# Fourier mixing gated with a dense Mish layer: fourteen additions of a loaded tile become accumulating transfers

## The chip, the core and the metric

The kernel runs on one core of a Trainium2 chip. The metric is device time in microseconds (us), median of several runs of the whole program. Engines are named as in the profile: PE (TensorE matmul), PEld (its weight load), DVE (VectorE), ACT (ScalarE), POOL (GpSimd), SP (SyncE). On-chip tiles live in SBUF; matmuls write to eight PSUM banks. Transfers are issued by SP (nearly all loads, and the stores of the output) and by POOL (the stores of intermediate results).

## The reference

```python
a = einsum("bsd,ed->bse", x, dft_hid_re);  b = einsum("bsd,ed->bse", x, dft_hid_im)
A = einsum("ts,bse->bte", dft_seq_re, a) - einsum("ts,bse->bte", dft_seq_im, b)
h = einsum("bsd,df->bsf", x, w1) + b1
B = einsum("bsf,fd->bsd", h * tanh(softplus(h)), w2)        # Mish
g = sigmoid((x * gate_w).sum(-1, keepdims=True))
out = g * A + (1 - g) * B
```

x is 2048 tokens by 640; the hidden size of the dense layer is 1728. All is float32.

## The kernel before

All results are kept transposed: rows are features (five blocks of 128, called d = 0 to 4), columns are tokens (four blocks of 512, called t = 0 to 3). A tile of 128 x 512 floats is 256 KB. Every matmul of float32 operands is three matmuls of operands that are split in a high and a low part (`mm3`, line 325); `operand` (line 313) makes the split, the high part on ACT (line 315), the low part on DVE (line 316). There are ten pairs of operand tiles (r0 to r9).

The stages come in this order. The sequence transform (`sq`) leaves u in DRAM. The hidden transform (`hd`) multiplies it by the gate g and leaves g y in DRAM: the scratch `ysc[d][t]`, twenty tiles, shown as `y` in the profile. The first dense layer leaves the activations in DRAM (`asc`, shown as `act`). The last stage (`ou`, weights `w2`) multiplies the activations, adds g y, and stores `out`. Each of these products is a 2 x 2 block scheme with seven block products in place of eight (class `Problem`, line 391), for two token blocks at a time, with the fifth feature block beside it:

- `first` computes the block product that others start from, and for the second pair of token blocks puts it by in DRAM (`aside`, shown as `po`) until it is needed;
- `second` runs the products called 22, s2 and s1 over six steps k, after a remainder of the contraction (`rest`);
- `third` runs 12, s3 and s4 over six steps, and gives the results.

The last stage has two such problems. In problem 0 (t = 0 and 1) the results leave PSUM in `done` and `give`, multiplied by 1 - g (`q`), and `plus` (line 541) then adds a loaded tile of g y to each of its ten results: line 543, a load and a DVE addition. In problem 1 (t = 2 and 3) the activations were scaled by 1 - g already, so g y is added on the way: `add_y` (line 474) adds it as a PSUM bank is emptied (six tiles), and four tiles are added to partial sums in SBUF that were read back from `po`: line 427 for the fifth block of t = 3, lines 455 to 457 for two tiles, and line 461 for the fifth block of t = 2. These four partial sums are then copied by ACT into a PSUM bank (`copy`, line 296), on which later matmuls accumulate. Additions are the helper `tt`, whose line is 288.

Nothing of the order is written out by hand but that of the matmuls. The program is collected as a graph (`Graph.add`), the matmuls in the order of the calls; `Graph.run` then plans the other engines by list scheduling: due times are worked back from the matmuls, each instruction has a modelled duration, and of the instructions that are ready the one that is due first goes next, if a tile can be granted from its pool (`FS`: 18 tiles f, to which the six tiles x are added when the stages that use them are through). A transfer is modelled as 2.2 us and its size at 370 KB per us. The result is one fixed order for each engine and each queue, and a tile for each value. On the chip every queue runs in that order: an instruction that waits holds up all behind it on its queue.

Of the kernel before, what the change touches and what calls it, by code (L numbers as in the profile page):

```python
# [12 lines left out]
OP = mybir.AluOpType  # L13

S, D, F = 2048, 640, 1728
P = 128
N = 512
# [202 lines left out]
def fnet_mish_gate(ctx: ExitStack, tc: tile.TileContext, xn, xt, c_re, c_im, wd_re, wd_im,  # L220
                   w1a, w1b, b1a, b1b, w2, gw, out):
    nc = tc.nc
# [10 lines left out]
    FS = Pool("f", [sb.tile([P, N], F32, name=f"f{i}") for i in range(NFS)])  # L233
# [11 lines left out]
    def scratch(name, n, rows=P):  # L245
        return [[dram(f"{name}{i}_{t}", rows) for t in range(TG)] for i in range(n)]

    usc, ysc = scratch("u", 2 * KD), scratch("y", KD)
# [6 lines left out]
    def whole(*vals):  # L255
        return [(v, None) for v in vals]

    def dve(emit, r, w, n=N, more=0.0):
        took = 0.15 + n / 960 + more
        return G.add("DVE", emit, r, w, took, took - 0.083)  # L260
# [5 lines left out]
    def dma(queue, emit, r, w, size):  # L266
        op = G.add(queue, emit, r, w, DELAY + size / RATE, 0.605 if queue == "SP" else 1.0)
        op.moves = size / RATE
        return op
# [3 lines left out]
    def load(pool, src, of=None, rows=P, cols=N, queue="SP"):  # L273
        v = Val(pool)
        dma(queue, lambda: ISSUE[queue].dma_start(v.t[:rows, :cols], src() if callable(src) else src),
            whole(of) if of else [], whole(v), rows * cols * 4)
        return v

    def load_of(pool, d, rows=P):
        return load(pool, lambda: d.t, d, rows)  # L280

    def store(d, v, rows=P, queue=None):
        queue = queue or STORES
        dma(queue, lambda: ISSUE[queue].dma_start(d.t, v.t[:rows]), whole(v), whole(d), rows * N * 4)  # L284

    def tt(o, a, b, op, cut=(slice(None),) * 3, rows=slice(None), n=N):
        (x, y, z) = cut
        dve(lambda: nc.vector.tensor_tensor(o.t[rows, x], a.t[rows, y], b.t[rows, z], op=op),  # L288
            whole(a, b), whole(o), n)

    def fresh(pool, a, b, op):
        o = Val(pool)
        tt(o, a, b, op)
        return o

    def copy(o, a, scale=1.0):
        act(lambda: nc.scalar.activation(o.t, a.t, AF.Copy, scale=scale), whole(a), whole(o))  # L297
        return o

    def to_sbuf(bank):  # L300
        return copy(Val(FS), bank)
# [11 lines left out]
    def operand(src, pool=None):  # L313
        r = Val(pool or R)
        act(lambda: nc.scalar.activation(r.t[0][:, :N], src.t[:, :N], AF.Copy), whole(src), [(r, 0)])  # L315
        dve(lambda: nc.vector.tensor_tensor(r.t[1][:, :N], src.t[:, :N], f32(r.t[0][:, :N]), op=OP.subtract),  # L316
            whole(src) + [(r, 0)], [(r, 1)])
        return r
# [12 lines left out]
    def product(banks, blocks, x, start, stop):  # L331
        for bank, b in zip(banks, blocks):
            mm3(bank, b, x, start, stop)

    def bank():
        return Val(psum)
# [3 lines left out]
    class Stage:  # L340
# [25 lines left out]
        def low(self, k):  # L366
            if k in self.XB:
                return
            f, g, t = load(X, self.row(k)[:, :N]), load(X, self.row(k + self.kh), cols=D), Val(X)
            if self.neg:  # L370
                copy(g, g, -1.0)
            tt(f, f, f, OP.subtract, (A2, B2, A2), n=2 * P)
            tt(t, g, f, OP.subtract, (A2, B2, A2), n=2 * P)
            tt(f, f, g, OP.subtract, (B2, B2, B2), n=2 * P)
            tt(t, g, t, OP.subtract, (B2, A2, A2), n=2 * P)
            self.top(k)
            if k // KD not in self.T2:
                self.T2[k // KD] = Val(W)
            b, c = self.XB[k], self.XT13[k] = Val(W), Val(W)
            split(self.XA[k], 3, t, 2 * P, 2 * P)  # L380
            split(c, 4, t, 0, P)
            split(self.T2[k // KD], k % KD, t, P, P)
            split(c, 0, f)
            split(b, 0, g, 0, D)

    def in_turn(kh, begin, between, end):
        order = [(p, k) for p in begin for k in (0, 1)]
        order += [(p, k) for k in range(2, kh - 2) for p in between]
        return order + [(p, k) for p in end for k in (kh - 2, kh - 1)]

    class Problem:
# [25 lines left out]
        def second(self, low):  # L417
            st, kh, t1, t2, y = self.st, self.st.kh, self.t1, self.t2, self.y
            own = {}
            if self.aside:  # L420
                self.p1 = [load_of(FS, d) for d in self.aside[:2]]
                self.d = load_of(FS, self.aside[2])
                self.a = [copy(bank(), v) for v in self.p1]
            d2 = self.d
            if y:
                d2 = y(4, t2)
                tt(d2, d2, self.d, OP.add)
            self.d2 = copy(bank(), d2)
            p4, b = [bank(), bank()], [bank(), bank()]
            opened = False  # L430
            if self.rest:
                e = [bank(), bank()]
                self.rest(t2, e + p4 + [self.d2], (2, 3, 0, 1, 4), 4)
                opened = True
                r22 = [self.add_y(v, y, 2 + j, t2) for j, v in enumerate(e)]
            for p, k in in_turn(kh, *[("22", "s2", "s1")] * 3):
                if p == "22":
                    low(k)
                    a22, a21, a11 = self.moving(t2, k + kh), self.moving(t2, k), self.moving(t1, k)
                    tt(a21, a21, a22, OP.add)  # L440
                    tt(a11, a21, a11, OP.subtract)
                    own.update({("22", k): a22, ("s1", k): a21, ("s2", k): a11})
                x = operand(own.pop((p, k)))
                if p == "22":
                    product(p4, st.blocks("t4", k), x, k == 0 and not opened, k == kh - 1)
                    product([self.d2], st.blocks("low5", k), x, False, k == kh - 1)
                elif p == "s2":
                    product(self.a, st.t2(k), x, False, k == kh - 1)
                else:
                    product(b, st.blocks("t1", k), x, k == 0, k == kh - 1)  # L450
                if k < kh - 1:
                    continue
                if p == "22":
                    self.p4 = [self.add_y(v, y, j, t2) for j, v in enumerate(p4)]
                    if y:
                        for j, v in enumerate(self.p1):
                            tt(v, v, y(j, t1), OP.add)
                    self.c = [copy(bank(), v) for v in self.p1]
                    if self.aside:
                        if y:  # L460
                            tt(self.d, self.d, y(4, t1), OP.add)
                        self.d1 = copy(bank(), self.d)
                elif p == "s2":
                    u2 = [self.add_y(v, y, 2 + j, t1) for j, v in enumerate(self.a)]
                else:
                    self.p5 = [to_sbuf(v) for v in b]
                    for v, u in zip(b, u2):
                        tt(v, v, u, OP.add)
                    if self.rest:
                        for v, r in zip(self.p5, r22):  # L470
                            tt(v, v, r, OP.add)
            self.b = b
# [67 lines left out]

        def plus(self, f, d, t):
            if self.st is fin and not self.y:
                tt(f, f, load_of(FS, ysc[d][t]), OP.add)
            self.finish(d, t, f)

        def end(self):
# [252 lines left out]
    def put_out(d, t, f, queue=None):  # L799
# [8 lines left out]
                  y=(lambda d, t: load_of(FS, ysc[d][t])) if tp else None,  # L808
# [78 lines left out]
```

## Time and profile before

| | us |
|---|---|
| median of 3 runs | 868.31 (867.33 to 868.6) |
| the profiled execution, its own time | 868.39 |
| its span, first to last instruction | 866.6 |
| PE busy | 859.3 |
| DVE busy | 679.0 |
| ACT busy | 463.1 |
| POOL busy | 69.7 |

The profile tells busy time by engine, groups of instructions, who waited for whom, the chain of work that ended last, and the instructions by time. Matmuls follow one another every 0.23 us while each is shown as 0.39 us long, as they overlap; an idle gap stands in square brackets with what ended it. A DMA issue is shown on its queue (SPq, POOLq, ACTq), and its landing is told in the view of DMA issues. The last stage runs from about 694 us to the end; its problem 0 ends, and problem 1 goes on to its `second` part, at about 788 us, and to its `third` part at 824 us.

### The profile page before, as it was taken

How to read it: one execution, taken by the hardware profiler on the slowest of the kernel's cores; microseconds unless marked ns; L12 is line 12 of the kernel's file. 1: busy time of each engine (PE TensorE's matmuls, PEld its weight loads, DVE VectorE, ACT ScalarE, POOL GpSimd, SP SyncE). 2: the span in 40 equal slices, each digit the busy share in tenths (PEclk: the TensorE clock that was granted, in tenths of full speed). 3: DMA queues.
4: the chain of work that ended last, by engine and by line, in shares of the span. 5: the costliest groups of instructions: out<-in, count | busy, mean ns of one | idle time of the engine just before them, and what ended most of it. 6: DMA issues, size and time to landing. Idle time of an engine off the chain costs nothing.

```text
span 866.6 us, 11980 instructions
## 1 busy us (share of the span) xinstructions
PE 859.3 (99%) x3772; PEld 709.0 (82%) x3772; DVE 679.0 (78%) x1213; ACT 463.1 (53%) x849; POOL 69.7 (8%) x132
## 2 busy tenths in 40 slices
PE   9999999999999999999999999999999999999998
PEld 7888888888888878888888888888888888887786
DVE  7999958876785577999999899925576897739991
ACT  7765536544553544667473666745655764521541
POOL 0000002001000200002002012111222100000000
PEclk9999999999999999999999999999999999999999
DMA  9976749564955565679975959455363778526943
GB/s 331 340 274 233 271 148 344 197 211 136 356 177 189 188 242 182 217 270 339 370 267 210 331 207 362 166 195 203 126 211 137 263 274 287 185 84 209 377 161 121
DMA packets 103231, 203.50 MB, mean 235 GB/s; under 512 B 12800, under 2 KB 15232, under 8 KB 103168
## 3 DMA queue, kind: packets, MB, share of 16 engines
q1 hardware_dynamic: 92912, 169.57, 57.1%
q0 software_dynamic: 10112, 33.04, 10.3%
q8 instruction: 29, 0.48, 0.2%
q14 instruction: 34, 0.28, 0.1%
q10 hardware_dynamic: 144, 0.13, 0.0%
HBM read 164.40 MB, written 38.29 MB: 234 GB/s over the span
## 4 chain that ended last, share of the span: by engine, by line
PE 96%; DVE 1%; DMA 1%; ACT 1%; issue 0%; ACTq 0%; DVEq 0%
PE ps L321 96%; DVE f L288 1%; DMA x<-po 1%; PE ps L744 0%; DMA out_dram<-f 0%; DVE x L288 0%; ACT ps L297 0%; ACT r5h L315 0%; DVE r9l L316 0%; DVE r7l L316 0%; ACT r4h L315 0%; ACT r9h L315 0%; ACT r3h L315 0%; DVE r1l L316 0%; ACT r6h L315 0%
## 5 line engine op out<-in xcount | busy, mean ns | idle before, releaser
L288 DVE TENSOR_TENSOR f<-f,f 128x512 f32<-128x512 f32 x311 | 209.1, 685 | 10.7 <-DMA f<-u 3.5
L288 DVE TENSOR_TENSOR f<-ps,f 128x512 f32<-128x512 f32 x101 | 66.0, 685 | 43.3 <-PE ps L321 43.0
L297 ACT ACTIVATE f<-ps 128x512 f32<-128x512 f32 x128 | 74.9, 595 | 38.9 <-PE ps L321 30.4
L284 POOL DMA_DIRECT2D u<-f x40 | 21.6, 543 | 322.7 <-DVE f L288 310.1
L315 ACT ACTIVATE r3h<-f 128x512 fp32r<-128x512 f32 x43 | 27.1, 629 | 30.0 <-PE ps L321 17.8
L315 ACT ACTIVATE r2h<-f 128x512 fp32r<-128x512 f32 x40 | 25.2, 631 | 32.4 <-PE ps L321 23.7
L579 ACT ACTIVATE f<-f,b1s 128x512 f32<-128x512 f32 x36 | 25.7, 723 | 29.1 <-DVE f L288 29.0
L316 DVE TENSOR_TENSOR r9l<-f,r9h 128x512 fp32r<-128x512 f32 x41 | 28.2, 688 | 14.8 <-ACT r9h L315 14.4
L315 ACT ACTIVATE r1h<-f 128x512 fp32r<-128x512 f32 x38 | 23.9, 630 | 29.2 <-PE ps L321 19.0
L284 POOL DMA_DIRECT2D act<-f x52 | 28.3, 545 | 133.6 <-DVE f L288 71.0
L315 ACT ACTIVATE r8h<-f 128x512 fp32r<-128x512 f32 x40 | 25.2, 631 | 25.4 <-PE ps L321 18.0
L315 ACT ACTIVATE r9h<-f 128x512 fp32r<-128x512 f32 x41 | 25.8, 628 | 23.2 <-PE ps L321 19.0
L315 ACT ACTIVATE r0h<-f 128x512 fp32r<-128x512 f32 x40 | 25.1, 628 | 23.8 <-PE ps L321 18.1
L316 DVE TENSOR_TENSOR r2l<-f,r2h 128x512 fp32r<-128x512 f32 x40 | 27.6, 689 | 12.3 <-ACT r2h L315 12.0
L316 DVE TENSOR_TENSOR r7l<-f,r7h 128x512 fp32r<-128x512 f32 x39 | 26.8, 688 | 12.8 <-ACT r7h L315 12.5
L315 ACT ACTIVATE r6h<-f 128x512 fp32r<-128x512 f32 x39 | 24.5, 629 | 22.7 <-PE ps L321 16.4
L315 ACT ACTIVATE r7h<-f 128x512 fp32r<-128x512 f32 x39 | 24.5, 629 | 22.6 <-PE ps L321 16.1
L315 ACT ACTIVATE r5h<-f 128x512 fp32r<-128x512 f32 x40 | 25.1, 629 | 20.0 <-PE ps L321 14.1
L316 DVE TENSOR_TENSOR r0l<-f,r0h 128x512 fp32r<-128x512 f32 x40 | 27.5, 688 | 10.5 <-ACT r0h L315 10.2
L316 DVE TENSOR_TENSOR r5l<-f,r5h 128x512 fp32r<-128x512 f32 x40 | 27.5, 688 | 10.2 <-ACT r5h L315 8.2
L316 DVE TENSOR_TENSOR r8l<-f,r8h 128x512 fp32r<-128x512 f32 x40 | 27.5, 688 | 9.8 <-ACT r8h L315 9.5
L315 ACT ACTIVATE r4h<-f 128x512 fp32r<-128x512 f32 x37 | 23.3, 629 | 21.4 <-PE ps L321 20.9
(1876 smaller groups left out, 2651.2 us busy)
## 6 DMA issues: line engine op xcount, KB each, us to landing
f<-in_c_re_dram SPq DMA_DIRECT2D x128, 256.0 KB, 4.4
f<-in_c_im_dram SPq DMA_DIRECT2D x128, 256.0 KB, 3.2
f<-act SPq DMA_DIRECT2D x81, 256.0 KB, 5.2
f<-u SPq DMA_DIRECT2D x80, 256.0 KB, 5.3
act<-f POOLq DMA_DIRECT2D x52, 256.0 KB, 3.1
f<-in_xt_dram SPq DMA_DIRECT2D x44, 256.0 KB, 5.0
u<-f POOLq DMA_DIRECT2D x40, 256.0 KB, 4.9
x<-in_xn_dram SPq DMA_DIRECT2D x25, 320.0 KB, 5.4
```

Of the source, the lines that this page charges most:

```text
L284: dma(queue, lambda: ISSUE[queue].dma_start(d.t, v.t[:rows]), whole(v), whole(d), rows * N * 4)
L288: dve(lambda: nc.vector.tensor_tensor(o.t[rows, x], a.t[rows, y], b.t[rows, z], op=op), whole(a, b), whole(o), n)
L297: act(lambda: nc.scalar.activation(o.t, a.t, AF.Copy, scale=scale), whole(a), whole(o))
L315: act(lambda: nc.scalar.activation(r.t[0][:, :N], src.t[:, :N], AF.Copy), whole(src), [(r, 0)])
L316: dve(lambda: nc.vector.tensor_tensor(r.t[1][:, :N], src.t[:, :N], f32(r.t[0][:, :N]), op=OP.subtract), whole(src) + [(r, 0)], [(r, 1)])
L321: G.add("PE", lambda: nc.tensor.matmul(bank.t, w.t[wn][:, k * P:k * P + P], x.t[xn_][:, :N], start, stop, skip_group_check=True), [(w, (k, ...
L579: act(lambda: nc.scalar.activation(o.t[rows], src.t[rows], AF.Mish, **more), whole(src, table) + whole(b1s) * bias, whole(o), more=0.1)
```

## The change

Fourteen additions of a tile that was loaded only for this are made by a transfer that adds what it reads to what is in the destination. The ten of `plus`, the two of line 457, and the ones of lines 427 and 461 are changed; the six of `add_y`, whose other addend is in PSUM, are as before. For the tile of line 427 the destination was the loaded g y, with a shared partial sum added to it; it is now a second load of the partial sum from `po`, to which g y is added. The planner models the new transfer as one of 1.5 times the size, issued by POOL.

```diff
+    def add_from(v, d):
+
+        dma("POOL", lambda: nc.gpsimd.dma_start(v.t, d.t, accum_op=OP.add), whole(v, d), whole(v), 1.5 * P * N * 4)
+
...
             if y:
-                d2 = y(4, t2)
-                tt(d2, d2, self.d, OP.add)
+                d2 = load_of(FS, self.aside[2])
+                add_from(d2, ysc[4][t2])
             self.d2 = copy(bank(), d2)
...
                         for j, v in enumerate(self.p1):
-                            tt(v, v, y(j, t1), OP.add)
+                            add_from(v, ysc[j][t1])
                     self.c = [copy(bank(), v) for v in self.p1]
                     if self.aside:
                         if y:
-                            tt(self.d, self.d, y(4, t1), OP.add)
+                            add_from(self.d, ysc[4][t1])
                         self.d1 = copy(bank(), self.d)
...
         def plus(self, f, d, t):
             if self.st is fin and not self.y:
-                tt(f, f, load_of(FS, ysc[d][t]), OP.add)
+                add_from(f, ysc[d][t])
             self.finish(d, t, f)
```

In the built program the order of the matmuls is the same; the other engines are planned anew. DVE has fourteen instructions fewer, SP thirteen transfers fewer, POOL fourteen more, all of them behind its last store of before. The orders of SP, ACT and DVE are the same as before up to problem 0's `third` part.

## The prediction

> **What bounds the kernel now.** I read the page's engine shares and its chain first, then PE's list of waits, then the stalls by time, then the last stage cut into stretches.
>
> ```profile
> span 866.6 us, 11980 instructions
> PE 859.3 (99%) x3772; PEld 709.0 (82%) x3772; DVE 679.0 (78%) x1213; ACT 463.1 (53%) x849; POOL 69.7 (8%) x132
> ...
> PE 96%; DVE 1%; DMA 1%; ACT 1%; issue 0%; ACTq 0%; DVEq 0%
> ```
>
> ```profile
> PE ps L744 <- DVE r9l L742: 2.0, 1, 2.0
> PE ps L321 <- DVE r1l L316: 0.4, 1, 0.4
> PE ps L321 <- ACT ps L297: 0.3, 1, 0.3
> PE ps L321 <- ACT r1h L315: 0.3, 1, 0.3
> PE ps L321 <- DVE r5l L316: 0.2, 1, 0.2
> ```
>
> ```profile
> 798.04 0.50 PE L321 MATMUL ps<-r5l,w11h 128*128 128x512 f32 x1 [0.23 <-DVE r5l L316]
> ...
> 806.36 0.51 PE L321 MATMUL ps<-r1h,w22h 128*128 128x512 f32 x1 [0.28 <-ACT r1h L315]
> ...
> 807.25 0.50 PE L321 MATMUL ps<-r1l,w22h 128*128 128x512 f32 x1 [0.38 <-DVE r1l L316]
> ```
>
> PE is busy in 859.3 of 866.6 us, so all idling of PE is 7.3 us: the 2.0 us wait at the start, the tail, and little between. The change touches the last stage, and there PE stands still three times, together 0.23 + 0.28 + 0.38 = 0.89 us. That is all that work taken from other engines can win.
>
> ```profile
> core 0: us, PE busy (x) PEld busy (x) DVE busy (x) ACT busy (x) POOL busy (x), PEclk, DMA share, GB/s
> 779.60:787.60 8.00, 8.00 (x37) 6.61 (x36) 8.00 (x14) 1.15 (x2) 0.00 (x0) 1.00 0.10 31
> 787.60:798.00 10.40, 10.21 (x45) 8.03 (x43) 10.21 (x18) 1.90 (x4) 0.00 (x0) 1.00 0.87 301
> 798.00:808.00 10.00, 9.21 (x36) 6.62 (x37) 7.04 (x12) 3.18 (x7) 0.00 (x0) 1.00 1.04 371
> 808.00:824.20 16.20, 16.20 (x73) 13.37 (x73) 15.89 (x27) 10.04 (x18) 0.00 (x0) 1.00 1.05 367
> 824.20:862.70 38.50, 38.43 (x170) 31.50 (x168) 24.36 (x40) 12.18 (x22) 0.00 (x0) 1.00 0.37 136
> 862.70:866.60 3.90, 0.00 (x0) 0.00 (x0) 0.42 (x1) 0.35 (x1) 0.00 (x0) 1.00 0.38 134
> ```
>
> The stretches tell why it stalls there and nowhere else. When problem 0 hands over to problem 1, DVE is full from 779.6 to 798 while DMA first lies idle (31 GB/s) and then runs full to 824 (371 GB/s). PE lives through that on operands made ahead, and runs out of them for a moment. The tail (3.90 us) has nothing that the change touches.
>
> ```profile
> 749.48 0.33 SPq L275 DMA_DIRECT2D f<-y  x1
> ...
> 779.60 1.29 DVE L288 TENSOR_TENSOR f<-ps,f 128x512 f32<-128x512 f32 x2 [2.12 <-PE ps L321]
> ...
> 796.11 0.60 ACT L297 ACTIVATE ps<-x 128x512 f32<-128x512 f32 x1 [14.03 <-DMA x<-po]
> ...
> 804.63 0.63 ACT L315 ACTIVATE r3h<-f 128x512 fp32r<-128x512 f32 x1 [1.45 <-DVE f L288]
> ```
>
> DMA idles for want of tiles: g y is loaded from 749.48 on, and each of its tiles stays taken until DVE has the result to which it is added, after 779.60. So the partial sum from po comes late, ACT stands 14.03 us for it, and the loads behind it hold the DVE addition that ACT awaits before 804.63. These end in the three stalls.
>
> **The change part by part.**
>
> ```profile
> L288 DVE TENSOR_TENSOR f<-f,f 128x512 f32<-128x512 f32 x52 | 35.0, 684 | 0.0
> ```
>
> *Removed from DVE*: 14 additions of 0.684 us, 9.6 us. On the path this counts only through the stalls: the ten of problem 0's results fall in 779.6 to 808, where DVE is full and PE runs short. The new order empties the banks without additions between, so DVE comes some six instructions sooner to problem 1's operands.
>
> *Removed from SP*: 14 loads of g y; one more load of po; 13 transfers fewer. The ten tiles that g y held are free for loads of problem 1. In the new order both po loads and the activations for the first three steps (and part of the fourth) stand ahead of the first store of a result; in the order of before they stand among the stores. So the wait of 14.03 us goes, the operands are early again, and I take all three stalls as gone: -0.89 us. What is late next is the start of `third`, below.
>
> ```profile
> 469.66 3.34 POOL L284 DMA_DIRECT2D y<-f  x6 [0.66 <-DVE f L288]
> ```
>
> ```profile
> 469.66:473.00 3.34, 3.34 (x17) 2.76 (x16) 3.34 (x7) 0.52 (x1) 3.24 (x6) 1.00 0.84 270
> ```
>
> *Added to POOL*: 14 issues. Six plain stores left it in 3.34 us, 0.56 each; 14 make 8 us on an engine that in all stretches above does nothing. The first (line 427's) is issued long before it is due. The next ten add to problem 0's results, the last three to problem 1's partial sums: in that order, on one queue.
>
> ```profile
> f<-act SPq DMA_DIRECT2D x65, 256.0 KB, 5.2
> ...
> f<-y SPq DMA_DIRECT2D x14, 256.0 KB, 4.7
> ...
> po<-f POOLq DMA_DIRECT2D x1, 256.0 KB, 6.5
> ```
>
> *The accumulating transfer itself* is in no row. These are the medians from issue to landing in the last stage: from below it is the load of g y, 4.7 us; from above, that load and then POOL's store, 4.7 + 6.5 = 11.2 us. It is nearest to the slow store, as its read of g y and of the tile can overlap: I take 6.5 us, and keep both ends. It does not lie on PE's path unless it is far longer:
>
> ```profile
> 811.92 0.39 PE L321 MATMUL ps<-r5h,w15h 128*128 128x512 f32 x1
> ```
>
> *The wait added to SP.* A store of a result now waits for the accumulating transfer, and loads stand behind it on SP. The first result is written by the fifth DVE instruction after 779.60, so at about 782.7 (they follow every 0.60 us); behind its store stands the third activation tile of step k = 3, whose matmuls (s2) begin at 811.92, or 811.0 without the stalls. Back from there: two DVE instructions of 0.68, one of ACT of 0.63 and a load of 5.2 us, so the transfer may take until 803.8, 21 us. The later stores have more room. At 6.5 us, or 11.2, this costs nothing; beyond 21 us each us costs one.
>
> The Trainium skill speaks against the change here: "DMA: Bandwidth & Descriptors", Rules for kernel authors, says that an accumulating transfer reads its destination and writes it later with nothing held between, so whatever touches the tile next must wait for its semaphore. That is the store's wait; by the same page's fit (Anatomy of one DMA), 2.0 us and the bytes at 436 KB per us, an estimate of 2.6 us for one would keep it as harmless.
>
> ```profile
> 823.95 1.06 ACT L297 ACTIVATE f<-ps 128x512 f32<-128x512 f32 x2
> 824.91 0.62 ACT L315 ACTIVATE r9h<-f 128x512 fp32r<-128x512 f32 x1
> ```
>
> ```profile
> 825.52 0.39 PE L321 MATMUL ps<-r3h,w0h 128*128 128x512 f32 x1
> ```
>
> *The waits added to ACT.* The copies of the partial sums into PSUM for `third` wait for the eleventh to thirteenth transfer after the first; POOL can issue these by 782.7 + 13 x 0.56 = 790, and the last is due at 825.52 - 0.89 = 824.6. But the new plan has ACT empty the two banks of s1 ahead of this last copy, while in the order of before all three copies stand ahead of that. By the rows: the banks take 823.95 to 824.91, a copy 0.60 us, so 825.51 against the matmul of 825.52 that needs it. With the semaphore I put 0.1 us.
>
> **The sum.** Span 866.6 - 0.89 + 0.1 = 865.8. The profiled execution took 868.39, 1.8 more than its span, so 867.6; the median of the runs shown is 0.08 below that execution: **867.5 us**. 0.2% of the time is 1.7 us, about what a measurement of this kernel tells from no change; a gain of 0.8 is inside it.
>
> **The rivals.**
>
> *A. Hidden anyway.* The stalls stay in another place: a load or an operand is as late as before, since DMA from 798 to 824 is full and the new transfers move 256 KB each as the old loads did. For it: only 0.89 us is in play. Against it: DMA is nearly idle at 779.6 to 787.6 and the tiles for using that time come free. It gives 868.3.
>
> *B. A slow queue (slower).* If the accumulating transfers go one after another at a pace of p us, the thirteenth ends at 782.7 + 13 p, and the last copy for `third` must be through at 824.6, so it must land by 823.9: p up to 3.2 us costs nothing, and beyond that each 0.1 us costs 1.3. At 3.5 us it is 3.9 us: 871.4; at 4.7 us (one after another, each like a load of g y), 19.5 us: 887. Against it: plain stores left POOL every 0.56 us and DMA moved 270 GB/s beside them, so these overlap; for it: no row shows how fast the adding path is. Also here: a single transfer over 21 us.
>
> *C. POOL held up by DVE.* DVE is full until 798, and if POOL's issue had to wait for that, the first transfer would begin at about 799 in place of 782.7, end at 805.5, the load behind it at 810.7 and its operand at 812.7, against 811.0: 1.7 us more than the forecast, 869.2. Against it is the stretch 469.66 to 473.00: six POOL issues while DVE was busy in all of it. The Trainium skill ("SBUF — State Buffer", Who interferes with whom) has such a rule: GpSimd is blocked by DVE where both want the shared port, though for a two-input addition it takes only reads to be held. The trace agrees that issues are not held.
>
> *D. Faster than the stalls allow.* It would need 1.7 us from start or tail, which are untouched.
>
> **How the numbers follow.** The forecast 0.55, A 0.23, B 0.17, C 0.02, D 0.03. So faster by over 0.2% 0.03, within it 0.80, slower 0.17. The range: from 867.4 less half a us of the runs' own spread, 866.9, to B at 3.5 us, 871.4; the likeliest alone has 866.9 to 868.1.
>
> **What would show it.** Right: no PE stall between 779 and 823; no wait of ACT for the po load; both po loads ahead of the first store of a result; far more than 31 GB/s at 779.6 to 787.6; ten accumulating transfers each landing in 4.7 to 11.2 us. Wrong: a PE stall near 824 with ACT waiting for a transfer from y (B), SP's stores issued long after DVE wrote their tiles and operands late at 811 (21 us), POOL idle with a ready tile while DVE works (C).

## The result and the profile after

The changed kernel takes 874.89 us (median of 6 runs, 873.73 to 876.05) against 868.25 us of the kernel before (6 runs): a ratio of 1.0076, with a 95% interval of 1.0067 to 1.0086. It is 6.6 us slower. The profiled execution took 875.2 us, with a span of 873.4. In the code, everything behind the new helper stands four lines lower: `mm3` is line 325, the copies of ACT line 301, the split 319 and 320, the new transfer 288.

The engine shares of the changed kernel:

```profile
span 873.4 us, 11965 instructions
PE 860.4 (99%) x3772; PEld 710.7 (81%) x3772; DVE 671.1 (77%) x1199; ACT 462.0 (53%) x849; POOL 81.8 (9%) x146
```

DVE lost 7.9 us and POOL gained 12.1, and PE still does the same 3772 matmuls. What changed is where PE stands. In the last stage (690 to 874 us) it waits once, and the timeline of PE has the place:

```profile
830.12 0.80 PE L325 MATMUL ps<-r3h,w0h 128*128 128x512 f32 x1 [5.95 <-ACT ps L301]
```

The three stalls of before are gone, and one of 5.95 us has come, at the start of `third` of problem 1. Its releaser is ACT's copy of a partial sum into PSUM. ACT's timeline shows what that copy stood behind:

```profile
824.53 0.63 ACT L319 ACTIVATE r8h<-f 128x512 fp32r<-128x512 f32 x1 [3.46 <-DVE f L292]
825.90 0.63 ACT L319 ACTIVATE r2h<-f 128x512 fp32r<-128x512 f32 x1 [0.74 <-DVE f L292]
827.97 0.63 ACT L319 ACTIVATE r4h<-f 128x512 fp32r<-128x512 f32 x1 [1.44 <-DMA f<-act]
828.51 0.58 ACT L301 ACTIVATE x<-ps 128x512 f32<-128x512 f32 x1
828.98 0.59 ACT L301 ACTIVATE f<-ps 128x512 f32<-128x512 f32 x1
829.46 0.60 ACT L301 ACTIVATE ps<-f 128x512 f32<-128x512 f32 x1
```

The copy (829.46) comes sixth. Ahead of it are the two emptied banks that the prediction had counted, and ahead of these the high parts of three operands, r8, r2 and r4, each waiting for work on a loaded activation. PE does not need these operands for the matmul of 830.12, which reads r3. The data of the copy were there much earlier: with one instruction moved, a run below makes the same copy at 822.21.

The chain of work that ended last names the loads behind it:

```profile
796.78 11.32 DMA f<-act
...
808.16 7.04 DMA f<-y
...
815.22 6.11 DMA x<-act
...
821.40 6.47 DMA f<-act
...
827.97 0.09 ACT r4h L319
```

So from 797 to 828 us the end hangs on transfers, one of them 11.32 us long. The stretches show why. Columns are as in the prediction:

```profile
779.60:787.60 8.00, 8.00 (x37) 6.64 (x36) 7.11 (x12) 3.54 (x7) 3.11 (x4) 1.00 0.22 54
787.60:798.00 10.40, 10.40 (x48) 8.61 (x47) 9.18 (x16) 2.82 (x5) 7.43 (x9) 1.00 1.09 218
798.00:808.00 10.00, 10.00 (x46) 8.29 (x45) 2.68 (x4) 2.42 (x4) 0.00 (x0) 1.00 1.10 262
...
823.99:830.12 6.13, 0.18 (x2) 0.01 (x1) 5.12 (x9) 3.41 (x7) 0.00 (x0) 0.85 1.05 327
830.12:835.27 5.15, 5.15 (x12) 4.06 (x13) 5.12 (x10) 2.70 (x5) 0.00 (x0) 0.52 1.05 385
```

The DMA engines are full from 787.6 to 808 (shares 1.09 and 1.10) and yet move only 218 and 262 GB/s, where the kernel before moved 301 and 371 in the same stretches at shares of 0.87 and 1.04. The view of the queues (740 us to the end) says what fills them. Columns are packets, MB and the share of the 16 engines' time; below them are issues with KB and the median time to landing:

```profile
q1 hardware_dynamic: 11580, 20.90, 45.9%
q0 software_dynamic: 2016, 3.67, 15.8%
...
f<-y POOLq DMA_DIRECT2D x10, 256.0 KB, 10.7
...
x<-y POOLq DMA_DIRECT2D x4, 256.0 KB, 6.9
```

The queue q0 holds the 14 accumulating transfers: 15.8% of 133.4 us is 21.1 us, 1.51 us of all 16 engines for each. The plain transfers of q1 (loads and stores by SP) take 61.2 us for 20.90 MB, or 0.77 us per 256 KB. By these rows an accumulating transfer of a tile costs the DMA engines twice what a plain one costs; the first experiment tests this.

The loss has a second part. In the last row of the stretches PE is busy throughout, but its granted clock is 0.52, with 12 matmuls in 5.15 us; the same stretch of the kernel before:

```profile
830.12:835.27 5.15, 5.15 (x24) 4.26 (x23) 5.09 (x9) 0.69 (x2) 0.00 (x0) 1.00 0.45 164
```

At 0.23 us each, the twelve matmuls would have taken 2.7 us, so 2.4 of the 5.15 us are lost. PE restarts slowly after the 5.95 us of standing. The Trainium skill ("TensorE: Matmul & The Clock Gate", Part 1: The HAM clock gate) says that the clock goes to half after an idle window of about 3.4 us and returns after about as long of work. The trace agrees in kind: 5.95 us of standing brought 0.52 for 5.15 us. Two runs below bear on the length of the idle window: with only the four partial sums changed, stalls of 1.43 and 0.31 us left the clock at 1.00 in every stretch of 2 us from 804 to 814; with one copy moved, stalls of 0.37 and 1.24 us, one matmul between them, were followed by a clock of 0.50, so there no single idle stretch of 3.4 us was needed.

The sum by the trace: the matmul of 830.12 would by the pace before it have come at 823.99, 6.13 us lost; with the 2.4 us of the half clock that is about 8.6. Against it stands what the removed stalls were worth. The same 111 matmuls, from the first one of w23h to the last one of w14l, before and then after:

```profile
793.90 0.39 PE L321 MATMUL ps<-r8h,w23h 128*128 128x512 f32 x1
...
821.22 0.39 PE L321 MATMUL ps<-r1h,w14l 128*128 128x512 f32 x1
```

```profile
794.76 0.39 PE L325 MATMUL ps<-r8h,w23h 128*128 128x512 f32 x1
...
819.69 0.39 PE L325 MATMUL ps<-r9h,w14l 128*128 128x512 f32 x1
```

They take 27.32 us before and 24.93 after: the change did win 2.4 us there. 8.6 - 2.4 = 6.2 us, beside a measured 6.6. (The profiled execution of the changed kernel also had a start 0.86 us longer, where nothing was changed; its span is 6.8 us longer.)

### The profile page after: what moved, and what is told of

Same layout as the page of the kernel before. It is cut to its first block, busy times and chain, and to the rows that moved or that the text cites. A ratio compares the mean times of both kernels' runs of the same rounds, so it can differ in the third digit from the quotient of the medians.

```text
span 873.4 us, 11965 instructions
## 1 busy us (share of the span) xinstructions
PE 860.4 (99%) x3772; PEld 710.7 (81%) x3772; DVE 671.1 (77%) x1199; ACT 462.0 (53%) x849; POOL 81.8 (9%) x146
## 4 chain that ended last, share of the span: by engine, by line
PE 93%; DMA 4%; DVE 2%; ACT 1%; issue 0%; SPq 0%; ACTq 0%; DVEq 0%
PE ps L325 93%; DMA f<-act 2%; DMA f<-y 1%; DVE f L292 1%; DMA x<-act 1%; DMA x<-in_xn_dram 1%; DVE x L292 1%; ACT r4h L319 0%; ACT f L301 0%; ACT ps L301 0%; SPq L275 0%; DVE r4l L320 0%; DVE r3l L320 0%; DVE r7l L320 0%; DVE r0l L320 0%
## 5 line engine op out<-in xcount | busy, mean ns | idle before, releaser
L292 DVE TENSOR_TENSOR f<-f,f 128x512 f32<-128x512 f32 x306 | 205.8, 685 | 17.0 <-DMA f<-u 5.9
L292 DVE TENSOR_TENSOR f<-ps,f 128x512 f32<-128x512 f32 x97 | 63.2, 684 | 40.5 <-PE ps L325 40.3
L319 ACT ACTIVATE r4h<-f 128x512 fp32r<-128x512 f32 x40 | 25.2, 630 | 28.6 <-PE ps L325 23.8
L320 DVE TENSOR_TENSOR r4l<-f,r4h 128x512 fp32r<-128x512 f32 x40 | 27.5, 688 | 12.5 <-ACT r4h L319 12.1
L319 ACT ACTIVATE r5h<-f 128x512 fp32r<-128x512 f32 x39 | 24.5, 629 | 21.1 <-PE ps L325 12.9
```

## The experiments

Four theories stand behind the expectations. *Theory 1*: the accumulating transfers take more DMA time, so the loads among and behind them come late. *Theory 2*: loads are late because on SP they stand behind stores that wait for the accumulation. *Theory 3*: the place of the last copy in ACT's order alone costs the time. *Theory 4*, which joins 1 and 3: the DMA time makes loads and operands late, and ACT's fixed order puts a copy that PE needs at once behind operands that it needs later. In the runs whose line numbers differ from these, only lines were added above.

### Plain transfers in the same order

The fourteen transfers of POOL are plain loads, with the same sizes and waits in the same order on every engine; the sums that they made are left out.

```diff
-        dma("POOL", lambda: nc.gpsimd.dma_start(v.t, d.t, accum_op=OP.add), whole(v, d), whole(v), 1.5 * P * N * 4)
+        dma("POOL", lambda: nc.gpsimd.dma_start(v.t, d.t), whole(v, d), whole(v), 1.5 * P * N * 4)
```

> The program of the changed kernel, instruction for instruction, but the fourteen transfers on GpSimd's queue are plain loads: what they load replaces the tile instead of being added to it, so g y is there and the partial sums and products under it are lost. Theory 1 (DMA time: an adding transfer takes the DMA engines twice as long as a plain one, 1.5 against 0.77 us, and ten come when the loads of problem 1 are due): 14 x 0.75 = 10 us of DMA time are freed, the stall of 5.95 us at the start of the last third part and the half clock behind it go, 866 to 867 us. Theory 2 (stores on SP wait for the adding transfers and hold up the loads behind them): the landings are shorter but the waits stay; the stall shrinks to 1 to 4 us, 869 to 872. Theory 3 (the last copy of a partial sum is placed too late in ACT's order): the order is the same, the stall stays at 5 to 6 us, 874.

Measured: 866.42 us (865.93 to 866.67), ratio 0.998 [0.997, 0.9989] to the kernel before. The chain that ended last has PE unbroken from 318 us on; the queue, the stretches and the two ACT rows that answer to those above:

```profile
318.50 542.23 PE ps L325 x2390
```

```profile
q0 software_dynamic: 1120, 3.67, 8.3%
```

```profile
787.60:798.00 10.40, 10.40 (x47) 8.62 (x46) 9.62 (x17) 3.04 (x6) 4.24 (x8) 1.00 0.97 341
798.00:808.00 10.00, 10.00 (x45) 8.27 (x45) 7.29 (x12) 4.59 (x9) 0.55 (x1) 1.00 1.05 407
```

```profile
820.82 0.61 ACT L319 ACTIVATE r4h<-f 128x512 fp32r<-128x512 f32 x1
...
822.82 0.59 ACT L301 ACTIVATE ps<-f 128x512 f32<-128x512 f32 x1
```

The same 3.67 MB take 8.3% of the engines' time in place of 15.8% (of a window 9 us shorter), DMA moves 341 and 407 GB/s, r4h is made 7.1 us sooner and the last copy 6.6 us sooner, in time. This is 8.5 us (874.9 - 866.4) between two kernels that differ in the kind of transfer alone. Theories 2 and 3 kept their causes in this kernel (the stores still wait for POOL's transfers, though these are shorter, and the copy stands in the same place), and no stall came. The copy's place alone does no harm, then; it takes the longer transfers as well.

### The planner told that each result lands 8 us later

The order of the work changes, not the work.

```diff
...
-                    end = dma + 0.1
+                    end = dma + 0.1 + op.late
...
-                add_from(f, ysc[d][t])
+                add_from(f, ysc[d][t]).late = 8.0
```

> As the changed kernel, but the planner believes that each of problem 0's ten adding transfers ends 8 us later than it did (about the 10.7 us measured), so that it places the stores of the results, which wait for them, further back on SP: six more loads stand ahead of the first store. Theory 1 (DMA time): the engines have as much to move in the same stretch, the stall stays at 4 us or more, 872 to 875. Theory 2 (SP's wait): the stall goes, 866 to 867. Theory 3 (ACT's order): it goes only if the new plan moves the last copy ahead of the late operand; as planned it stays, 872 to 875.

Measured: 866.75 us (866.28 to 867.48), ratio 0.9984 [0.9975, 0.9993]. ACT's rows, and the one stall of PE:

```profile
820.06 1.20 ACT L302 ACTIVATE ps<-f 128x512 f32<-128x512 f32 x2 [1.36 <-DVE f L293]
822.38 0.63 ACT L320 ACTIVATE r8h<-x 128x512 fp32r<-128x512 f32 x1 [1.12 <-DVE x L293]
825.65 0.63 ACT L320 ACTIVATE r2h<-f 128x512 fp32r<-128x512 f32 x1 [2.64 <-DVE f L293]
826.19 1.07 ACT L302 ACTIVATE f<-ps 128x512 f32<-128x512 f32 x2
827.14 0.63 ACT L320 ACTIVATE r4h<-f 128x512 fp32r<-128x512 f32 x1
```

```profile
831.00 0.50 PE L326 MATMUL ps<-r9l,w0h 128*128 128x512 f32 x1 [0.46 <-DVE r9l L321]
```

The edit was meant to get the loads out from behind the stores. On SP six loads do now go ahead of the first store (786.43 to 793.55), and the time is the one that theory 2 expected. But the operands are little earlier for it: r8h comes 2.2 us sooner than in the changed kernel (822.38, before 824.53), r2h and r4h only 0.3 and 0.8 us (825.65 and 827.14). The plan also moved the last copy ahead of all three (the second of the two at 820.06). With the copy early, and the operands nearly as late, 8.1 us are back. The time alone doesn't decide between the theories; the rows fit theory 3 or 4 better than theory 2. The run with one copy moved, below, gives the copy's share, 5.8 us; the stores' later place may have a part in the other 2.3.

### The fifth block by load and DVE, and only the four partial sums

Two runs undo parts of the change: the first only line 461's addition, the second the ten of `plus`.

```diff
-                            add_from(self.d, ysc[4][t1])
+                            tt(self.d, self.d, y(4, t1), OP.add)
```

> As the changed kernel, but the fifth block's partial sum of t = 2 (line 461), for whose copy PE stood still, gets its g y by a load and a DVE addition as before. Theory 3 (the place and the transfer of this one copy): the stall goes, 866 to 867. Theories 1 and 2 (loads late, by DMA time or by SP's wait): the loads are as late, and PE stands for the next operand instead, that of s4, some 4 us; 871 to 874.

```diff
-                add_from(f, ysc[d][t])
+                tt(f, f, load_of(FS, ysc[d][t]), OP.add)
```

> One part of the change alone: the four additions to partial sums of problem 1 are adding transfers, the ten additions to problem 0's results are loads and DVE additions as before. Theory 1 (DMA time): only 4 x 0.75 = 3 us more of DMA time, one of them long before, 867 to 869. Theory 2 (SP's wait): no store waits for an adding transfer, 866 to 868. Theory 3 (ACT's order): the last copy still waits for its adding transfer, up to 874.

Measured: 867.68 us (866.59 to 868.27), ratio 0.9994 [0.9984, 1.0003], and 869.88 us (869.41 to 871.9), ratio 1.0021 [1.0011, 1.003]. Neither run decides between the theories: the first is 0.7 us above what theory 3 expected and 3.3 below the others, the second lies above theories 1 and 2 and only within theory 3's "up to 874". In the first, the planner puts the last copy ahead of r8h (the second of two copies from 821.12), and PE stands only later, first row below. In the second, no tiles come free, and PE stalls where it did before, longer, the other two rows:

```profile
834.00 0.50 PE L325 MATMUL ps<-r7l,w12h 128*128 128x512 f32 x1 [0.97 <-DVE r7l L320]
```

```profile
807.37 0.50 PE L325 MATMUL ps<-r1h,w22h 128*128 128x512 f32 x1 [1.43 <-ACT r1h L319]
808.17 0.50 PE L325 MATMUL ps<-r1l,w22h 128*128 128x512 f32 x1 [0.31 <-DVE r1l L320]
```

The four alone only lose, so the gain of the change is with the ten. Whether it comes from the tiles that these free or from the work that DVE is spared, no run separates. In the first run, with the last copy ahead of the operands, the large loss does not come.

### One copy moved

The order of the changed kernel, with one instruction moved: the last copy goes ahead of five others on ACT.

```diff
...
+    def moved(self):
+        op = self.last_copy
+        at = self.seq.index(op)
+        to = [i for i, o in enumerate(self.seq[:at]) if o.engine == "ACT"][-5]
...
+        self.seq.insert(to, self.seq.pop(at))
...
```

> The program of the changed kernel with one ACT instruction in another place: the last copy of a partial sum into PSUM (the one PE stood 5.95 us for) is moved ahead of five operand and bank instructions, the late operands r8h, r2h and r4h among them. Every other queue is as it was. Theory 4, formed after the first four runs (the adding transfers' double DMA time makes the loads late, and ACT's fixed order puts the copy, which has its data by about 823, behind operands that wait for these loads): PE begins the third part on time and then meets the late operands themselves, 1 to 3 us, too short for the clock to fall: 867 to 869.5. Theory 2 (stores on SP hold the loads): the same, since the loads stay where they are. Theory 3 alone (nothing is wrong but the copy's place): no stall, 865.5 to 866.5.

Measured: 869.1 us (868.32 to 871.37), ratio 1.0013 [1.0004, 1.0023]. ACT's rows and PE's stalls:

```profile
822.21 0.60 ACT L314 ACTIVATE ps<-f 128x512 f32<-128x512 f32 x1 [1.70 <-DMA f<-y]
...
827.49 0.63 ACT L332 ACTIVATE r4h<-f 128x512 fp32r<-128x512 f32 x1 [1.31 <-DMA f<-act]
```

```profile
831.25 0.50 PE L338 MATMUL ps<-r9h,w0h 128*128 128x512 f32 x1 [0.37 <-ACT r9h L332]
...
832.99 0.50 PE L338 MATMUL ps<-r9l,w0h 128*128 128x512 f32 x1 [1.24 <-DVE r9l L333]
```

```profile
834.00:836.00 2.00, 2.00 (x6) 1.60 (x5) 1.94 (x4) 0.00 (x0) 0.00 (x0) 0.50 1.05 392
```

One instruction is worth 5.8 us (874.9 - 869.1), and `third` begins on time. But the operands are nearly as late as before, and PE stands for r9 at 831 and 833. The expectation took such stalls to be too short for the clock to fall, and in the profiled execution it fell: the last row, in the columns of the stretches, has 0.50 from 834 to 836. That execution took 870.34 us, above the median; the runs spread from 868.32 to 871.37. Theory 3 alone (865.5 to 866.5) is out: the late loads, with what they do to the clock, cost 2.7 us more than plain ones even then (869.1 - 866.4). Theory 4 holds by its time. Theory 2 was expected to give the same here, so this run does not tell these two apart; the run of only the ten does.

### The stores moved back on SP

The ten stores of results go back on SP, each to just ahead of the next use of its tile. A second run also moves the copy.

```diff
...
+    def moved(self):
+        for op in self.outs[9::-1]:
+            at = self.seq.index(op)
+            to = next(i for i in range(at + 1, len(self.seq)) if self.tiles(op) & self.tiles(self.seq[i]))
+            self.seq.insert(to - 1, self.seq.pop(at))
...
```

> The program of the changed kernel with the ten stores of problem 0's results moved back on SP, each to just before the next use of its tile (up to eighteen places), so that the loads behind them no longer wait for the adding transfers. ACT, DVE and POOL run in the order of the changed kernel. Theory 2 (SP's wait): the loads come early and the stall goes, 866 to 867.5. Theory 4 (DMA time and ACT's order): what the engines have to move in the stretch is the same, most of the stall stays, 871 to 874.5.

> Both moves together: the copy ahead on ACT, the ten stores back on SP. Theory 4: the late operands come somewhat earlier than with the copy's move alone, 866 to 868. Theory 2: as with the stores' move alone, 866 to 867.5. If any of the three is the whole, it equals that one's run.

Measured: 884.8 us (884.02 to 887.04), ratio 1.0195 [1.0179, 1.021], and with the copy moved 883.94 us (882.53 to 885.5), ratio 1.0181 [1.0164, 1.0197]. All theories missed this. SP's timeline of the first of the two:

```profile
791.24 0.63 SPq L296 DMA_DIRECT2D out_dram<-x  x1
802.76 0.32 SPq L287 DMA_DIRECT2D x<-act  x1
```

The store now stands right ahead of the load that overwrites its tile, and that load waits 11 us for accumulation and store. The edit took one wait of SP away and put a longer one in its place, so it does not test theory 2. It does show what the distance between a store and the next use of its tile is worth here: 9.9 us in the order of the changed kernel (884.8 - 874.9), 14.8 with the copy moved (883.9 - 869.1).

### Only the ten

The ten of `plus` by accumulating transfers, the four partial sums by load and DVE as before.

```diff
-                d2 = load_of(FS, self.aside[2])
-                add_from(d2, ysc[4][t2])
+                d2 = y(4, t2)
+                tt(d2, d2, self.d, OP.add)
...
-                            add_from(v, ysc[j][t1])
+                            tt(v, v, y(j, t1), OP.add)
...
-                            add_from(self.d, ysc[4][t1])
+                            tt(self.d, self.d, y(4, t1), OP.add)
```

> The other part of the change alone: the ten additions to problem 0's results are adding transfers, the four to partial sums of problem 1 are loads and DVE additions as before. Theory 4: 7.5 us more DMA time in the same stretch, but no copy waits for an adding transfer and the plan is another: 866.5 to 870, by where the copies stand in ACT's order. Theory 2: ten stores still wait: 870 to 875.

Measured: 867.08 us (865.96 to 867.6), ratio 0.9986 [0.9977, 0.9996]. All three copies stand ahead of r8h, and PE has one stall of 0.3 us:

```profile
819.83 1.20 ACT L301 ACTIVATE ps<-f 128x512 f32<-128x512 f32 x2 [1.36 <-DVE f L292]
821.93 0.63 ACT L319 ACTIVATE r8h<-f 128x512 fp32r<-128x512 f32 x1 [0.90 <-DVE f L292]
```

All ten waiting stores are in this kernel, in front of loads on SP, and it is faster than the kernel before. Theory 2 (870 to 875) is out as the main cause of the loss.

### A truer price in the planner, and the ten with a later landing

Theory 4 says that what decides is ACT's order. The first run tells the planner what the transfers were seen to take, and the plan that comes of it puts the copy still further back; the second joins the two cures, with the four partial sums as in the run before.

```diff
...
-        dma("POOL", lambda: nc.gpsimd.dma_start(v.t, d.t, accum_op=OP.add), whole(v, d), whole(v), 1.5 * P * N * 4)
+        op = dma("POOL", lambda: nc.gpsimd.dma_start(v.t, d.t, accum_op=OP.add), whole(v, d), whole(v), 2.1 * P * N * 4)
+        op.late = 4.0
```

> The change with the planner told what an accumulating transfer was seen to take: 2.1 times the size in place of 1.5, and 4 us more until it lands. All three now stand truer in the plan; its answer is to put the last copy of a partial sum (the fifth block of t = 2) still further back on ACT, behind five operand splits (r8h, r2h, r4h, r5h, r0h) and r7h in place of three. Theory 4 (the copy stands on ACT behind operands whose loads come late): PE stands at the start of third at least as long as the 5.95 us of the changed kernel, with one row of ACT's copy as its releaser, and the half clock follows; time 874 to 880. Theory 1 alone (DMA time): a plan with true costs asks loads in a better order, time 867 to 872. That a truer price in the planner cures it is what one would hope for; theory 4 says it does not, since the copy's late data is what the plan now foresees.

```diff
...
-                            add_from(self.d, ysc[4][t1])
+                            tt(self.d, self.d, y(4, t1), OP.add)
...
-                add_from(f, ysc[d][t])
+                add_from(f, ysc[d][t]).late = 8.0
```

> The ten additions of results by accumulating transfers, the four partial sums by load and DVE as before, and the planner told that each of the ten lands 8 us later. On ACT all three copies stand ahead of r2h and r4h, the last one behind r8h. Theory 4: no stall of PE above 1 us, no half clock; time 866 to 867.5, so at or below both single cures (867.08 and 866.75). If the wait of loads behind the stores on SP were what mattered (theory 2), the planned lateness should win over the ten alone by more than 1 us, below 866.

Measured: 875.75 us (874.0 to 876.25), ratio 1.0081 [1.0067, 1.0095], and 866.17 us (865.7 to 866.77), ratio 0.9976 [0.9966, 0.9987]. In the first, ACT's last copy is behind r7h, and PE has the stall of the changed kernel, 0.3 us longer:

```profile
828.50 0.63 ACT L321 ACTIVATE r7h<-f 128x512 fp32r<-128x512 f32 x1
829.03 0.58 ACT L303 ACTIVATE ps<-x 128x512 f32<-128x512 f32 x1
```

```profile
829.67 0.80 PE L327 MATMUL ps<-r3h,w0h 128*128 128x512 f32 x1 [6.28 <-ACT ps L303]
```

In the second, PE runs unbroken to the end of its work:

```profile
318.31 542.05 PE ps L326 x2390
```

Both came as theory 4 said. Knowing the true price did not help the planner, which saw the copy's data come late and let operands go first. The joined version is, by its ratio, 2.1 us faster than the kernel before (1.7 by the medians, 867.84 and 866.17). It has the lowest median of all here, though its interval overlaps those of the two single cures; 2.1 us is close to the 2.4 us that the removed stalls are worth.

## Why the prediction was wrong

The forecast was 867.5 us with a range to 871.4; 874.89 is outside it, and on the side given 0.17. By its own steps:

- *The stalls go (-0.89).* Right in kind. Two `po` loads stand ahead of the first store, at 759.85, and the wait of 14.03 us on ACT is gone; the `po` load for the last copy came behind five stores, at 806.20. The three stalls are gone too, but they were worth 2.4 us, not 0.89. The idle in brackets begins at the end that is shown for the matmul ahead, while matmuls otherwise start every 0.23 us. The first row below, of the kernel before, is the one ahead of the stall at 798.04 with its bracket of 0.23: the two starts are 0.73 us apart, so 0.50 was lost. The second, of the changed kernel, is the two `po` loads.

```profile
797.31 0.50 PE L321 MATMUL ps<-r5h,w11h 128*128 128x512 f32 x1
```

```profile
759.85 1.68 SPq L275 DMA_DIRECT2D f<-po  x2
```

- *DMA's idle stretch is used.* Mostly wrong: the stretch from 779.6 to 787.6 has 54 GB/s, beside 31, not far more.
- *POOL's issues (0.56 us each, hidden).* Mis-sized and hidden. The issue of an accumulating transfer took 1.02 us in the median, that of a plain one by POOL 0.55. In the view of the tile y (instruction, then the least, median and greatest ns), the changed kernel and then the one with plain transfers:

```profile
L288 POOL DMA_DIRECT2D f<-y x10: 857/1022/1672, 750.0 to 815.1; - x10
```

```profile
L288 POOL DMA_DIRECT2D f<-y x10: 548/548/553, 749.8 to 806.0; - x10
```

- *The transfer itself (6.5 us, bounds 4.7 and 11.2).* The medians by tile, 6.9 and 10.7, lie within the bounds; single ones took from 4.3 to 15.0 us, so the sign that each lands in 4.7 to 11.2 failed. A further step was missing: it priced the transfer by its time to landing, and the engines' time that it takes from the loads beside it was nowhere in the sum. Fourteen cost 0.74 us more each (1.51 - 0.77), 10 us of DMA time, most of it where DMA was full already, and the operands behind it came 7 us late. By the fit of the Trainium skill that the prediction quotes ("DMA: Bandwidth & Descriptors", Anatomy of one DMA) a transfer takes an estimated 2.6 us; none here was that short. The same page (Issuing engines are not separate DMA queues) says that transfers of all issuing engines share the same 16 DMA engines; the rows of the stretches agree.
- *The wait on SP (room of 21 us, nothing).* No stall came at s2, as said. What the waiting stores add is not isolated: with plain transfers, which the stores also wait for but less long, there was no loss, and the ten with their waiting stores were faster than before.
- *The waits on ACT (+0.1 us).* This is the step that failed. The place was right: the last copy, the start of `third`, the copy behind two emptied banks. The sum counted these two and took their times from the rows of before. It did not count the three operand splits that also stand ahead of the copy in the new order, nor ask when their loads would land. They made the +0.1 into 6.1 us of standing and 2.4 us of half clock; with the copy moved ahead of them and nothing else, 5.8 us came back.
- *The rivals.* B named the place and the sign, at 0.17, but by another mechanism: thirteen transfers one after another. In the trace the last one was issued at 815.12 because its `po` load had come late, not because the queue was slow. C did not come: POOL issued while DVE was busy. A is out, since the stalls went.

What stays open: how much the stores' waits on SP add by themselves, since the run that was to take them away put another wait in their place, and the later stores of another run came together with an earlier copy.

## What to carry to other kernels

When a transfer takes over an addition, price it twice: by its landing, and by the time that it takes from the DMA engines, above all where they are already full. When a change replans an engine's order, go through every instruction ahead of the one that PE waits for and ask when its data land in the new kernel, not in the old; here one copy behind three late operands decided between 875 and 869 us. Two cheap cures helped here: to move the urgent instruction ahead (869.1 us, still no gain on the kernel before), or to make only the ten transfers whose results no copy waits for (867.1).

## What the runs showed of the hardware

An accumulating transfer of 256 KB from DRAM to SBUF took 1.51 us of the 16 DMA engines, a plain one 0.77; its issue on POOL took 0.85 us or more, that of a plain one 0.55; and it came in more packets (2016 in place of 1120 for the fourteen). In the same two stretches DMA, full or nearly so, moved 218 and 262 GB/s with them, 341 and 407 GB/s with plain ones. A stall of PE of 5.95 us cost another 2.4 us by a clock of 0.52 over the next 5.15 us; in the run with one copy moved, stalls of 0.37 and 1.24 us close together were followed by a clock of 0.50 from 834 to 836, and in another run stalls of 1.43 and 0.31 us left it at 1.00. And three stalls shown as 0.89 us were worth 2.4 us.
